# WKV attention, FFN and routed experts on one core: the work ahead of block 0 in another order

## The chip, the cores and the metric

The kernel runs on one core of a Trainium2 chip. The metric is the device time of the program in microseconds, as the median of three runs. TensorE is called PE in the profile, its weight loads PEld, VectorE DVE, ScalarE ACT, GpSimd POOL, and SyncE, which only issues loads and stores here, SP. Each engine works through its own instructions strictly in the order in which the program lists them.

## The reference

Three stages follow one another. First a linear attention with decay, for 4 batches, 8 heads, 768 steps and heads of 48:

```
cur   = outer(u * k[t], v[t])
y[t]  = r[t] @ (state + cur)
state = w[:, None] * state + outer(k[t], v[t])
```

Its output, 3072 tokens of width 384, goes through a gated FFN, `(silu(x @ w_gate) * (x @ w_val)) @ w_out` with an inner width of 1536, whose weights come as 64-bit floats. Last, a router picks one of 8 experts for each token (argmax over `x @ w_gate`), and the expert's `relu(x @ w1) @ w2`, inner width 1024, is scaled by the softmax probability and a sigmoid gate.

## The kernel before, in words

The 3072 tokens are 24 tiles of 128, and three tiles form a block, so that there are 8 blocks. A program written out by hand fixes the order of the instructions on every engine. Ahead of block 0 stands a prologue: it sets constants, builds the tables of the powers of w, computes the attention of tiles 0 to 2, and decodes the FFN weights of the first of twelve groups f. Then `b_block` runs the FFN of each block over its twelve groups, and slots between the groups hold the attention of the next block's tiles, in block 0 also the decoding of the further weight groups. After the blocks come the eight experts.

The steps of the prologue, with the names that the change touches:

- `setup_consts` fills tables and zeros (`wT`, `uT`, `uw`, `rev`, `kr3`, `ident`, `triu`, `mask`, `ones`, `shf`) and starts the first loads. `kr3[i]` takes keys and receptances of tile i, `krT` those of tile 3; they are zeroed first, since a load fills 48 of every 64 partitions. SP issues the loads in the program's order, and a load whose target isn't free holds up those behind it.
- `decay_tables` builds `WT`, the table of powers of w and 1/w, and `uw`, on DVE.
- `a_scale(i)` (L322) multiplies keys and receptances by `WT` on DVE. `a_scores(i)` (L376) forms the scores of a tile in two PSUM banks. `a_same(i)` forms the diagonal: a product on POOL (L325) and four thin sums on TensorE (L328) into bank 7, which `a_same_copy` (L333) takes out. `a_diag(i)` spreads it into a diagonal matrix, on ACT with eight multiplications (L355) or on POOL with one (L357). `a_mask(i)` (L381) puts the masked scores over it, on DVE.
- `a_out_mm(i)` multiplies by the values (L403). The last pair of heads comes first; ACT takes it out (L410), and products with `shf` (L400, the fold products) add it to the other three pairs. `a_out_ev(i)` takes the result out as a rounded part on ACT (L423) and a rest on DVE (L424), which together are `xT`, the FFN's input.
- `conv_steps(f)` decodes the weights of group f in three steps of three DVE instructions (L224 to L226); `conv_a(f)` runs all three. `conv_b(f)` splits them into a rounded part on ACT (L242) and a rest on POOL (L243). `gate_a` transposes the output weights for the router (L251, copy L253).
- `key_table` builds the table `Wk` by which keys enter the state: a product on POOL (L179), four transposes on TensorE (L181), a copy on ACT (L182). `a_keys` (L366) applies it.
- `b_up` (L507) and `b_down` (L526) are the FFN's products. Block 0 starts with the 18 products of `b_up` for group 0.

Most fp32 products show as two records in the trace.

Of the kernel before, what the change touches and what calls it, by code (L numbers as in the profile page):

```python
# [8 lines left out]
F32 = mybir.dt.float32  # L9
# [42 lines left out]
def kernel(  # L52
# [3 lines left out]
    rkv_d: bass.AP,  # L56
    w_d: bass.AP,
    u_d: bass.AP,
    w64_d: bass.AP,
    g_d: bass.AP,  # L60
    w12_d: bass.AP,
# [24 lines left out]
    bad = cst.tile([P, 2 + NF], F32, name="bad")  # L86
    badb = cst.tile([P, 1], BF16, name="badb")
    flag = cst.tile([P, 1], I32, name="flag")
    wT = cst.tile([P, 4], F32, name="wT")
    uT = cst.tile([P, 4], F32, name="uT")  # L90
    uw = cst.tile([P, 4, 2], F32, name="uw")

    right = ctx.enter_context(ExitStack())
# [20 lines left out]
    def bc(ap, axis, shape):  # L114
        return ap.unsqueeze(axis).to_broadcast(shape)
# [4 lines left out]

    def setup_consts():
        dve.memset(wT, 1.0)
        dve.memset(rev, 0.0)
        act.activation(out=rev, in_=rev, func=AF.Silu)
        dve.memset(uT, 0.0)
        dve.memset(uw, 0.0)
        dve.memset(kr3[0], 0.0)
        pool.memset(kr3[1], 0.0)
        for j in range(2):
            sp.dma_start(  # L130
                out=wT[64 * j : 64 * j + HD, :],
                in_=w_d.rearrange("(p j) d -> j d p", j=2)[j],
            )
        a_load_kr(0)
        for j in range(2):
            sp.dma_start(out=uT[64 * j : 64 * j + HD, :], in_=u_d.rearrange("(p j) d -> j d p", j=2)[j])
        dve.memset(kr3[2], 0.0)
        make_identity(nc, ident)
        pool.memset(triu, 1.0)
        pool.affine_select(  # L140
            out=triu, in_=triu, compare_op=ALU.is_gt, fill=0.0, base=0,
            pattern=[[1, P]], channel_multiplier=-1,
        )
        pool.tensor_copy(out=mask, in_=triu)
        pool.memset(ones, 1.0)
        pool.memset(cnt, 0.0)
        pool.memset(spare[4][:, 0 : 6 * P], 0.0)
        for c in range(KC):
            pool.tensor_copy(
                out=shf[:, c].rearrange("s (j m) -> s j m", j=2)[:, :, HD:64],  # L150
                in_=ident.rearrange("s (j m) -> s j m", j=2)[:, :, 16 * c : 16 * c + 16],
            )

    def pair(t, o, step, n):
        return bass.AP(tensor=t.tensor, offset=t.offset + o, ap=[t.ap[0], [P, 4], [step, 2], [1, n]])
# [18 lines left out]
            q = slice(64 * j, 64 * j + 64)  # L174
            dve.tensor_tensor(out=uw[q, :, j], in0=uT[q], in1=pw[q, 0, :, 0], op=ALU.mult)

    def key_table():
        wk2 = kp.rearrange("s h d -> s (h d)").rearrange("s (p t) -> s p t", p=4)
        pool.tensor_tensor(out=wk2, in0=WkT, in1=bc(pw[:, 0, :, 7], 2, [P, 4, P]), op=ALU.mult)  # L179
        for p in range(4):  # L180
            pe.transpose(bank[7][:, p * P : (p + 1) * P], wk2[:, p, :], ident)  # L181
        act.copy(  # L182
            out=Wk.rearrange("s (h d) -> s h d", h=NH),
            in_=bank[7].rearrange("s (h d) -> s h d", h=NH)[:, :, 0:HD],
        )
# [135 lines left out]
        t = kr3[i] if i < 3 else krT  # L321
        dve.tensor_tensor(out=t, in0=t, in1=WT, op=ALU.mult)  # L322

    def a_same(i):
        pool.tensor_tensor(out=pr3[i], in0=kr3[i][:, 0], in1=kr3[i][:, 1], op=ALU.mult)  # L325
        m = bank[7][:, i * 8 : (i + 1) * 8].rearrange("s (j p) -> s p j", j=2)
        for p in range(4):
            pe.matmul(m[:, p], pr3[i][:, p], uw[:, p], start=True, stop=True)  # L328
        a = apool.tile([P, NH], F32, tag="a3", name="a3", bufs=3)
        att[i]["a"] = a  # L330

    def a_same_copy(i, on_act):
        (act.copy if on_act else dve.tensor_copy)(out=att[i]["a"], in_=bank[7][:, i * 8 : (i + 1) * 8])  # L333
# [482 lines left out]
    with tc.manual_schedule():  # L816
# [6 lines left out]
        next_w(1)  # L823
        for i in range(3):
            a_load_part(i, 1)
        sp.dma_start(out=ub, in_=u_d.rearrange("h d -> (h d)").partition_broadcast(P))
        next_w(2)
        sp.dma_start(out=G, in_=g_d)
        decay_tables()
        sc = ((0, 1), (2, 3), (4, 6))  # L830
        for i in range(3):
            a_scale(i)
            a_scores(i, sc[i])
            a_same(i)
        a_same_copy(0, True)
        a_diag(0, True)
        steps = conv_steps(0)
        steps[0]()
        a_same_copy(1, False)
        a_same_copy(2, False)  # L840
        a_diag(1, False)
        a_diag(2, True)
        a_mask(0, sc[0])
        a_out_mm(0, 0, (3,))
        steps[1]()
        conv_b(0, (GV,))
        a_mask(1, sc[1])
        a_out_mm(1, 1, (3,))
        a_out_mm(0, 0, (0, 1, 2))
        a_mask(2, sc[2])  # L850
        a_out_mm(2, 2, (3,))
        a_out_mm(1, 1, (0, 1, 2))
        a_out_ev(0, 0)
        steps[2]()
        a_out_mm(2, 2, (0, 1, 2))
        a_out_ev(1, 1)
        a_out_ev(2, 2)
        gate_a(0)
        conv_b(0, (OUT,))
        key_table()  # L860
        pool.memset(krT, 0.0)
        for i in range(3):
            a_keys(i)
        for b in range(NB):
            pool.memset(Sst[b], 0.0)
        a_load(3)
        a_load_kr(3)
        next_w(3)
        next_w(4)
        conv_a(1)  # L870
        next_w(5)
        a_bonus(3)
        decay_bounds()
# [250 lines left out]
def _layout(inputs):  # L1124
    import numpy as np

    def tiles(a):
        return np.asarray(a).reshape(NB, NH, TPB, P, HD)

    def feat(a):  # L1130
        a = tiles(a).reshape(NB, 4, 2, TPB, P, HD)
        return a.transpose(0, 3, 2, 5, 1, 4).reshape(NT, 2, HD, 4, P)

    def tok(a):
        return tiles(a).transpose(0, 2, 3, 1, 4).reshape(NT, P, DM)

    def word(a):
        return np.ascontiguousarray(a).view(np.int64)

    rows = np.empty((KC, P), dtype=np.int64)  # L1140
    for c in range(KC):
        for j in range(2):
            rows[c, 64 * j : 64 * j + HD] = HD * (2 * c + j) + np.arange(HD)
            rows[c, 64 * j + HD : 64 * j + 64] = HD * (6 + j) + 16 * c + np.arange(16)
    w64 = np.empty((NF, P, FW), dtype=np.int64)
    for i, name in enumerate(("moe_w_gate", "moe_w_val")):
        a = word(inputs[name])[rows].reshape(KC, P, NF, P)
        w64[:, :, i * KC * P : (i + 1) * KC * P] = a.transpose(2, 1, 0, 3).reshape(NF, P, KC * P)
    w64[:, :, 2 * KC * P :] = word(inputs["moe_w_out"]).reshape(NF, P, DM)
    g = np.concatenate([inputs["moe2_w_gate"], inputs["moe2_w_output_gate"]], axis=1)  # L1150
    g = np.ascontiguousarray(g.reshape(KC, P, 16).transpose(1, 0, 2))
    w1 = np.asarray(inputs["moe2_w1"]).reshape(NE, KC, P, NEF, P).transpose(0, 2, 3, 1, 4)
    w2 = np.asarray(inputs["moe2_w2"]).reshape(NE, NEF, P, DM).transpose(0, 2, 1, 3)
    w12 = np.ascontiguousarray(np.concatenate([w1.reshape(NE, P, NEF, DM), w2], axis=3))
    return {
        "krT": np.ascontiguousarray(np.stack([feat(inputs["k"]), feat(inputs["r"])], axis=3)),
        "rkv": np.ascontiguousarray(np.stack([tok(inputs[n]) for n in "rkv"], axis=2)),
        "w": np.ascontiguousarray(inputs["w"]), "u": np.ascontiguousarray(inputs["u"]),
        "w64": w64, "g": g, "w12": w12,
    }  # L1160

# [20 lines left out]
```

## Time and profile before

| What | Value |
|---|---|
| median of 3 runs | 872.16 us (870.61 to 872.62) |
| the profiled execution's own time | 870.71 us |
| its span | 869.0 us |
| busy share of the span | PE 95%, PEld 92%, DVE 52%, ACT 31%, POOL 30% |
| PE's busy tenths in the first four of 40 slices | 5, 7, 7, 8 (then 8, 8, 9 and nearly always 9) |

The span is the time from the first to the last instruction of the profiled execution. A slice is a fortieth of it, 21.7 us, so the prologue is about the first two. A busy share is an average over stages with different limits: what decides in the prologue has to be read from the timelines of the engines there, which give for each group of instructions its start, its length, and the idle time of the engine before it with what ended that idle time.

### The profile page before, as it was taken

The page shows a single profiled execution, that of the slowest core. Times are in us where ns is not written, and L with a number is a line of the kernel's source. Part 1 is how long each engine was busy: PE and PEld are TensorE (multiplying, and loading weights), DVE is VectorE, ACT ScalarE, POOL GpSimd, SP SyncE. Part 2 cuts the span into 40 slices and gives each one's busy share as a digit, 9 for nine tenths or more (in the row PEclk, how much of TensorE's full clock was granted, in tenths as well). Part 3 has the DMA queues.
Part 4 walks back from the last instruction along what each step waited for, and adds up shares of the span by engine and source line. Part 5 has one row for each costly group of instructions (what it writes and reads, how often), then busy time and mean ns, then how long its engine had stood idle before and what let it go on. Part 6 is the DMA issues. An engine that isn't in the chain of part 4 may idle for free.

```text
span 869.0 us, 13916 instructions
## 1 busy us (share of the span) xinstructions
PE 828.9 (95%) x5451; PEld 797.9 (92%) x5451; DVE 456.1 (52%) x946; ACT 271.1 (31%) x591; POOL 262.4 (30%) x237
## 2 busy tenths in 40 slices
PE   5778889999999999999999999999999999999996
PEld 4377879999999999999999999899999999999996
DVE  5497792444456455455545535234575655555541
ACT  0433432211222222212211222223354444444432
POOL 4286565324244245245243312010110210121022
PEclk9999989999999999999999999999999999999999
DMA  8053432681323323323333210410295443434200
GB/s 279 31 209 128 182 109 60 186 216 48 118 87 127 112 100 129 114 101 128 114 101 129 60 46 19 147 51 22 101 355 165 135 162 117 165 136 167 84 25 35
DMA packets 30424, 104.30 MB, mean 120 GB/s; under 512 B 5591, under 2 KB 15377, under 8 KB 27280
## 3 DMA queue, kind: packets, MB, share of 16 engines
q1 hardware_dynamic: 27024, 93.78, 33.3%
q0 software_dynamic: 3328, 9.56, 2.9%
q8 instruction: 45, 0.74, 0.3%
q14 instruction: 27, 0.22, 0.1%
HBM read 85.25 MB, written 16.41 MB: 117 GB/s over the span
## 4 chain that ended last, share of the span: by engine, by line
PE 83%; DVE 6%; issue 2%; ACT 2%; DMA 1%; SPq 1%; POOL 1%; POOLq 0%; DVEq 0%; ACTq 0%
PE bank L507 31%; PE bank L526 17%; PE bank L721 12%; PE bank L738 12%; PE bank L376 2%; PE bank L403 2%; PE bank L389 2%; DVE bank L225 1%; DVE bank L224 1%; PE bank L686 1%; PE bank L752 1%; DVE cv L226 1%; SPq L428 1%; DVE s L516 1%; PE bank L440 1%
## 5 line engine op out<-in xcount | busy, mean ns | idle before, releaser
L507 PE MATMUL bank<-xT,W 128*128 128x384 f32 x1728 | 330.3, 341 | 1.6 <-DMA xT<-stage 1.6
L507 PEld LDWEIGHTS bank<-xT,W 128*128 128x128 f32 x1728 | 304.9, 189 | 5.5 <-DMA xT<-stage 2.5
L526 PE MATMUL bank<-W,h 128*128 128x400 f32 x864 | 177.5, 350 | 0.0
L526 PEld LDWEIGHTS bank<-W,h 128*128 128x128 f32 x864 | 157.1, 191 | 0.6 <-issue 0.2
L518 ACT CAST h<-s 128x384 fp32r<-128x384 f32 x96 | 49.2, 513 | 324.8 <-DVE s L516 324.8
L516 DVE TENSOR_TENSOR s<-s,bank 128x384 f32<-128x384 f32 x96 | 53.1, 554 | 162.0 <-PE bank L507 148.9
L738 PE MATMUL bank<-hd,wf 128*128 128x416 f32 (+1 forms) x576 | 114.1, 344 | 0.0
L738 PEld LDWEIGHTS bank<-hd,wf 128*128 128x128 f32 x576 | 104.5, 189 | 0.6 <-DVE hd L725 0.2
L760 POOL DMA_INDIRECT out_dram<-yo,ix x32 | 34.1, 1067 | 201.5 <-DVE yo L756 175.3
L357 POOL TENSOR_TENSOR at<-ident,a 128x1024 f32<-128x1024 f32 x19 | 36.0, 1897 | 148.6 <-PE bank L507 118.6
L519 DVE TENSOR_TENSOR h<-s,h 128x384 fp32r<-128x384 f32 x84 | 53.0, 631 | 48.6 <-ACT h L518 48.6
L725 DVE SCALAR_TENSOR_TENSOR hd<-bank,hd 128x416 fp32r<-128x416 f32 (+1 forms) x64 | 36.6, 573 | 77.1 <-ACT hd L724 77.1
L670 DVE TENSOR_TENSOR wf<-raw,wf 128x768 fp32r<-128x768 f32 x64 | 61.2, 957 | 7.0 <-ACT wf L669 1.2
L515 ACT ACTIVATE s<-bank 128x384 f32<-128x384 f32 x96 | 47.2, 491 | 47.7 <-PE bank L507 47.6
L721 PE MATMUL bank<-xd1h,wf 128*128 128x416 f32 x192 | 58.2, 360 | 0.0
L724 ACT ACTIVATE hd<-bank 128x416 fp32r<-128x416 f32 (+1 forms) x64 | 32.3, 505 | 82.3 <-PE bank L721 81.8
L588 POOL DMA_INDIRECT xs<-rows,slot x24 | 23.7, 987 | 113.5 <-DVE slot L586 51.5
L669 ACT CAST wf<-raw 128x768 fp32r<-128x768 f32 x64 | 52.8, 825 | 0.0
L381 DVE COPY_PREDICATED at<-mask,bank 128x512 f32<-128x512 int32 x42 | 28.5, 734 | 38.6 <-POOL at L357 35.3
L721 PE MATMUL bank<-xd0h,wf 128*128 128x416 f32 x144 | 43.8, 362 | 0.0
L243 POOL TENSOR_TENSOR W<-cv,W 128x1152 fp32r<-128x1152 f32 (+2 forms) x14 | 32.2, 2304 | 20.3 <-ACT W L242 20.3
L721 PEld LDWEIGHTS bank<-xd1h,wf 128*128 128x128 f32 x192 | 36.1, 189 | 0.4
(178 smaller groups left out, 936.9 us busy)
## 6 DMA issues: line engine op xcount, KB each, us to landing
raw<-in_w_dram SPq DMA_DIRECT2D x36, 768.0 KB, 4.4
raw<-in_w_dram SPq DMA_DIRECT2D x22, 1152.0 KB, 7.5
rkv<-in_rkv_dram SPq DMA_DIRECT2D x21, 576.0 KB, 5.5
krT<-in_krT_dram SPq DMA_DIRECT2D x42, 192.0 KB, 3.4
xs<-zt SPq DMA_DIRECT2D x32, 197.0 KB, 5.6
xr<-xs SPq DMA_DIRECT2D x6, 591.0 KB, 5.7
spare<-in_w_dram SPq DMA_DIRECT2D x2, 1152.0 KB, 8.2
xT<-stage SPq DMA_DIRECT2D x42, 48.0 KB, 2.1
```

Source lines behind the costliest of these rows:

```text
L357: pool.tensor_tensor(out=af, in0=bc(ident, 1, [P, NH, P]), in1=bc(a, 2, [P, NH, P]), op=ALU.mult)
L507: pe.matmul(ps[i], W[f][:, wl, o : o + P], x[:, xl, c, :], start=(c == 0 and n == 0), stop=(c == KC - 1 and n == 2),)
L515: act.activation(out=s, in_=g, func=AF.Silu)
L516: dve.tensor_tensor(out=s, in0=s, in1=v, op=ALU.mult)
L518: act.copy(out=h[:, 0], in_=s)
L519: (pool if blk == 0 else dve).tensor_tensor(out=h[:, 1], in0=s, in1=h[:, 0].bitcast(F32), op=ALU.subtract)
L526: pe.matmul(bank[t][:, 0 : DM + 16], h[:, hl, t * P : (t + 1) * P], W[f][:, wl, 2 * KC * P :], start=(f == 0 and n == 0), stop=(f == NF - ...
L669: act.copy(out=wf[:, 0], in_=raw[:, f])
L670: dve.tensor_tensor(out=wf[:, 1], in0=raw[:, f], in1=wf[:, 0].bitcast(F32), op=ALU.subtract)
L721: pe.matmul(ps, wf[:, wl, c * P : (c + 1) * P], xd[xl][:, c, 0:n], start=(i == 0), stop=(i == 3 * KC - 1))
L725: dve.scalar_tensor_tensor(h[:, 1, 0:n], ps, 0.0, h[:, 0, 0:n].bitcast(F32), ALU.max, ALU.subtract)
L738: pe.matmul(bank[c][:, 0:n], wf[:, wl, o : o + P], h[:, hl, 0:n], start=(f == 0 and i == 0), stop=(f == NEF - 1 and i == 2),)
```

## The change

The order of the prologue's instructions is changed on each engine. w and u come in one array `wu` and in two loads instead of four. The zeros of `krT` and of the states `Sst` are set at the start instead of ahead of block 0; the loads of tile 3 are moved ahead with them. `key_table` is cut in two, and both parts stand before the first value products. The decoding of weight group 1 is spread over the prologue, where it followed it. `pe_warm` is new: it multiplies the table of ones by itself, 384 columns at a time, into a part of bank 7, and nothing uses the results, 24 times at the start and 10 times between the scores.

```diff
@@ -56,6 +56,7 @@
     rkv_d: bass.AP,
     w_d: bass.AP,
     u_d: bass.AP,
+    wu_d: bass.AP,
     w64_d: bass.AP,
     g_d: bass.AP,
     w12_d: bass.AP,
@@ -86,8 +87,8 @@
     bad = cst.tile([P, 2 + NF], F32, name="bad")
     badb = cst.tile([P, 1], BF16, name="badb")
     flag = cst.tile([P, 1], I32, name="flag")
-    wT = cst.tile([P, 4], F32, name="wT")
-    uT = cst.tile([P, 4], F32, name="uT")
+    wuT = cst.tile([P, 2, 4], F32, name="wuT")
+    wT, uT = wuT[:, 0], wuT[:, 1]
     uw = cst.tile([P, 4, 2], F32, name="uw")
 
     right = ctx.enter_context(ExitStack())
@@ -120,20 +121,16 @@
 
     def setup_consts():
         dve.memset(wT, 1.0)
+        dve.memset(uT, 0.0)
+        for j in range(2):
+            sp.dma_start(out=wuT[64 * j : 64 * j + HD], in_=wu_d[j])
+        dve.memset(kr3[0], 0.0)
         dve.memset(rev, 0.0)
         act.activation(out=rev, in_=rev, func=AF.Silu)
-        dve.memset(uT, 0.0)
+        pool.memset(ones, 1.0)
+        a_load_kr(0)
+        pool.memset(kr3[1], 0.0)
         dve.memset(uw, 0.0)
-        dve.memset(kr3[0], 0.0)
-        pool.memset(kr3[1], 0.0)
-        for j in range(2):
-            sp.dma_start(
-                out=wT[64 * j : 64 * j + HD, :],
-                in_=w_d.rearrange("(p j) d -> j d p", j=2)[j],
-            )
-        a_load_kr(0)
-        for j in range(2):
-            sp.dma_start(out=uT[64 * j : 64 * j + HD, :], in_=u_d.rearrange("(p j) d -> j d p", j=2)[j])
         dve.memset(kr3[2], 0.0)
         make_identity(nc, ident)
         pool.memset(triu, 1.0)
@@ -142,7 +139,6 @@
             pattern=[[1, P]], channel_multiplier=-1,
         )
         pool.tensor_copy(out=mask, in_=triu)
-        pool.memset(ones, 1.0)
         pool.memset(cnt, 0.0)
         pool.memset(spare[4][:, 0 : 6 * P], 0.0)
         for c in range(KC):
@@ -150,6 +146,13 @@
                 out=shf[:, c].rearrange("s (j m) -> s j m", j=2)[:, :, HD:64],
                 in_=ident.rearrange("s (j m) -> s j m", j=2)[:, :, 16 * c : 16 * c + 16],
             )
+        pool.memset(krT, 0.0)
+        for b in range(NB):
+            pool.memset(Sst[b], 0.0)
+
+    def pe_warm(n, b=7):
+        for _ in range(n):
+            pe.matmul(bank[b][:, P:], ones, bc(ones, 1, [P, 3, P]), start=True, stop=True)
 
     def pair(t, o, step, n):
         return bass.AP(tensor=t.tensor, offset=t.offset + o, ap=[t.ap[0], [P, 4], [step, 2], [1, n]])
@@ -174,9 +177,12 @@
             q = slice(64 * j, 64 * j + 64)
             dve.tensor_tensor(out=uw[q, :, j], in0=uT[q], in1=pw[q, 0, :, 0], op=ALU.mult)
 
-    def key_table():
-        wk2 = kp.rearrange("s h d -> s (h d)").rearrange("s (p t) -> s p t", p=4)
+    wk2 = kp.rearrange("s h d -> s (h d)").rearrange("s (p t) -> s p t", p=4)
+
+    def key_table_a():
         pool.tensor_tensor(out=wk2, in0=WkT, in1=bc(pw[:, 0, :, 7], 2, [P, 4, P]), op=ALU.mult)
+
+    def key_table_b():
         for p in range(4):
             pe.transpose(bank[7][:, p * P : (p + 1) * P], wk2[:, p, :], ident)
         act.copy(
@@ -321,13 +327,14 @@
         t = kr3[i] if i < 3 else krT
         dve.tensor_tensor(out=t, in0=t, in1=WT, op=ALU.mult)
 
-    def a_same(i):
+    def a_same_a(i):
         pool.tensor_tensor(out=pr3[i], in0=kr3[i][:, 0], in1=kr3[i][:, 1], op=ALU.mult)
+
+    def a_same_b(i):
         m = bank[7][:, i * 8 : (i + 1) * 8].rearrange("s (j p) -> s p j", j=2)
         for p in range(4):
             pe.matmul(m[:, p], pr3[i][:, p], uw[:, p], start=True, stop=True)
-        a = apool.tile([P, NH], F32, tag="a3", name="a3", bufs=3)
-        att[i]["a"] = a
+        att[i]["a"] = apool.tile([P, NH], F32, tag="a3", name="a3", bufs=3)
 
     def a_same_copy(i, on_act):
         (act.copy if on_act else dve.tensor_copy)(out=att[i]["a"], in_=bank[7][:, i * 8 : (i + 1) * 8])
@@ -823,51 +830,60 @@
         next_w(1)
         for i in range(3):
             a_load_part(i, 1)
+        next_w(2)
         sp.dma_start(out=ub, in_=u_d.rearrange("h d -> (h d)").partition_broadcast(P))
-        next_w(2)
         sp.dma_start(out=G, in_=g_d)
+        a_load(3)
+        a_load_kr(3)
+        pe_warm(24)
         decay_tables()
         sc = ((0, 1), (2, 3), (4, 6))
         for i in range(3):
             a_scale(i)
-            a_scores(i, sc[i])
-            a_same(i)
+            a_same_a(i)
+        steps = conv_steps(0) + conv_steps(1)
+        a_scores(0, sc[0])
+        pe_warm(4)
+        a_scores(1, sc[1])
+        a_same_b(0)
         a_same_copy(0, True)
         a_diag(0, True)
-        steps = conv_steps(0)
+        pe_warm(3)
+        a_scores(2, sc[2])
+        a_same_b(1)
+        a_same_copy(1, True)
+        pe_warm(3)
+        a_same_b(2)
+        key_table_a()
         steps[0]()
-        a_same_copy(1, False)
-        a_same_copy(2, False)
-        a_diag(1, False)
-        a_diag(2, True)
-        a_mask(0, sc[0])
-        a_out_mm(0, 0, (3,))
         steps[1]()
         conv_b(0, (GV,))
+        a_diag(1, True)
+        a_mask(0, sc[0])
+        a_same_copy(2, False)
+        a_diag(2, False)
+        key_table_b()
+        a_out_mm(0, 0, (3,))
+        steps[2]()
+        conv_b(0, (OUT,))
         a_mask(1, sc[1])
         a_out_mm(1, 1, (3,))
         a_out_mm(0, 0, (0, 1, 2))
         a_mask(2, sc[2])
         a_out_mm(2, 2, (3,))
+        a_out_ev(0, 0)
         a_out_mm(1, 1, (0, 1, 2))
-        a_out_ev(0, 0)
-        steps[2]()
+        steps[3]()
+        a_out_ev(1, 1)
+        steps[4]()
         a_out_mm(2, 2, (0, 1, 2))
-        a_out_ev(1, 1)
+        gate_a(0)
+        steps[5]()
         a_out_ev(2, 2)
-        gate_a(0)
-        conv_b(0, (OUT,))
-        key_table()
-        pool.memset(krT, 0.0)
         for i in range(3):
             a_keys(i)
-        for b in range(NB):
-            pool.memset(Sst[b], 0.0)
-        a_load(3)
-        a_load_kr(3)
+        next_w(4)
         next_w(3)
-        next_w(4)
-        conv_a(1)
         next_w(5)
         a_bonus(3)
         decay_bounds()
@@ -1137,6 +1153,7 @@
     def word(a):
         return np.ascontiguousarray(a).view(np.int64)
 
+    wu = np.stack([inputs["w"], inputs["u"]])
     rows = np.empty((KC, P), dtype=np.int64)
     for c in range(KC):
         for j in range(2):
@@ -1156,6 +1173,7 @@
         "krT": np.ascontiguousarray(np.stack([feat(inputs["k"]), feat(inputs["r"])], axis=3)),
         "rkv": np.ascontiguousarray(np.stack([tok(inputs[n]) for n in "rkv"], axis=2)),
         "w": np.ascontiguousarray(inputs["w"]), "u": np.ascontiguousarray(inputs["u"]),
+        "wu": np.ascontiguousarray(wu.reshape(2, 4, 2, HD).transpose(2, 3, 0, 1)),
         "w64": w64, "g": g, "w12": w12,
     }
 
```

## Rows read from the trace of the kernel before

**Rows 1.** The page's first line.
```profile
span 869.0 us, 13916 instructions
...
```

**Rows 2.** Chain that ended last, 0 to 140 us: start us, us, what.
```profile
...
43.56 1.01 POOL kp L179
...
45.74 5.22 PE bank L507 x18
...
55.37 0.36 DVE S L454
...
126.83 2.07 PE bank L376 x14
...
```

**Rows 3.** Timeline of DVE, 0 to 75 us: start, us, instruction, idle before and releaser.
```profile
...
8.23 2.36 DVE L322 TENSOR_TENSOR spare<-spare,WT 128x1024 f32<-128x1024 f32 x2
10.87 1.94 DVE L322 TENSOR_TENSOR spare<-spare,WT 128x1024 f32<-128x1024 f32 x1 [0.27 <-DMA spare<-in_krT_dram]
13.39 0.56 DVE L224 TENSOR_SCALAR bank<-raw 128x384 int32<-128x384 int32 x1 [0.59 <-DMA raw<-in_w_dram]
...
21.49 0.24 DVE L333 COPY a<-bank 128x8 f32<-128x8 f32 x2 [6.35 <-ACT a L333]
...
26.32 2.55 DVE L381 COPY_PREDICATED spare<-mask,bank 128x512 f32<-128x512 int32 x4
...
41.29 0.56 DVE L424 TENSOR_TENSOR xT<-bank,xT 128x384 fp32r<-128x384 f32 x1 [3.42 <-ACT xT L423]
...
46.98 0.45 DVE L188 TENSOR_TENSOR wT<-wT,pw 128x4 f32<-128x4 f32 x1
...
```

**Rows 4.** Timeline of TensorE's products, 0 to 75 us.
```profile
...
9.52 2.08 PE L376 MATMUL bank<-spare 64*128 64x128 f32 x16 [9.52 <-DVE spare L322]
11.78 1.87 PE L328 MATMUL bank<-uw,spare 128*128 128x2 f32 x8 [0.19 <-POOL spare L325]
...
27.09 1.28 PE L403 MATMUL bank<-spare 128*48 128x128 f32 x4 [1.62 <-DVE spare L381]
...
40.66 0.90 PE L251 MATMUL bank<-ident,cv 128*128 128x128 f32 x3
...
45.39 5.57 PE L507 MATMUL bank<-xT,W 128*128 128x384 f32 x18
...
54.82 1.85 PE L507 MATMUL bank<-xT,W 128*128 128x384 f32 x9
...
60.02 1.16 PE L376 MATMUL bank<-krT 64*128 64x128 f32 x16
...
65.52 0.55 PE L251 MATMUL bank<-ident,cv 128*128 128x128 f32 x3 [2.56 <-DVE at L381]
66.63 0.90 PE L259 MATMUL bank<-G,gt 128*128 128x16 f32 x6 [0.57 <-ACT gt L253]
...
```

**Rows 5.** Windows: length, busy of PE, PEld, DVE, ACT, POOL, PEclk, DMA share, GB/s.
```profile
...
28.00:32.00 4.00, 4.00 (x20) 2.32 (x20) 0.87 (x2) 0.52 (x2) 1.50 (x1) 1.00 0.01 4
...
65.00:70.00 5.00, 3.92 (x17) 3.66 (x18) 4.76 (x9) 2.06 (x5) 4.62 (x4) 0.73 0.00 2
...
```

**Rows 6.** Timeline of SP's queue, 0 to 75 us: issues of loads.
```profile
...
3.07 0.91 SPq L136 DMA_DIRECT2D uT<-in_u_dram  x2
...
45.49 0.79 SPq L308 DMA_DIRECT2D krT<-in_krT_dram  x2
...
```

**Rows 7.** Timeline of POOL, 0 to 75 us.
```profile
...
9.55 5.62 POOL L325 TENSOR_TENSOR spare<-spare 128x512 f32<-128x512 f32 x3 [4.88 <-DVE spare L322]
...
44.51 0.95 POOL L861 MEMSET krT<- 128x1024 f32 x1
...
49.28 1.92 POOL L865 MEMSET S<- 128x512 f32 x4
...
```

**Rows 8.** Timeline of ACT, 0 to 75 us.
```profile
...
21.56 4.78 ACT L355 ACTIVATE spare<-ident,a 128x128 f32<-128x128 f32 x16
...
40.78 0.48 ACT L423 CAST xT<-bank 128x384 fp32r<-128x384 f32 x1 [3.50 <-PE bank L403]
...
```

## The prediction

> **What bounds the kernel now.** I read the page first, then the chain of waits, then the timeline of each engine over the first 75 us, and last the windows for the clock. The span is 869.0 us and the profiled execution took 870.71 us, so 1.7 us lie around the span [rows 1]; the median of the three runs is 872.16, which is 1.45 above it. From about 127 us on TensorE carries the chain nearly alone. Ahead of that the reader should see one handover: the chain runs through the key table on POOL (43.56) to TensorE's first product of block 0 at about 45.4, through its 18 products, and on to DVE at 55.37 [rows 2]; from there DVE (decoding weights) carries most of it until TensorE takes over at 126.83. So block 0 cannot start before 45.4, and every microsecond by which it starts earlier on TensorE and on DVE is one off the end, as long as nothing in the block has a due time of its own. Its weight loads follow buffers that DVE frees, so they move along.
>
> Before 45.4 the engines mostly wait for one another. DVE waits 6.35 us ahead of the copies at 21.49 and 3.42 us ahead of 41.29 [rows 3]. TensorE's first product is at 9.52, and its products of the prologue are slow: 16 records of the scores take 2.08 us there and 1.16 us at 60.02; the 18 up-products take 5.57 us (0.31 each) at 45.39, against 1.85 for 9 (0.21, its tail counted) at 54.82 [rows 4]. That is TensorE at 1.2 against 2.4 GHz, the two levels of its clock. The clock column shows 1.00 in the window 28 to 32 [rows 5], but there the product durations contradict it, and I go by the durations. The long run is 27.09 to 41.56 (40.66 + 0.90) [rows 4]: value and fold products almost without a pause for 14.5 us, and no sign that the clock rose.
>
> **The change part by part.**
>
> *Loads.* w and u come in two loads instead of four. Two issues of together 0.91 us leave SP's queue [rows 6], and what is behind them lands up to 0.9 earlier. DVE waits 0.27 and 0.59 for those loads [rows 3], 0.86 in all; between nothing and 0.86 I take 0.6: the first decode step starts at 12.8 instead of 13.39. The krT load of tile 3, which stands at 45.49 in SP's queue behind POOL's memset [rows 6], and with it all later weight loads, is issued some 30 us earlier. That costs the path nothing and is no gain, since no row of DVE's timeline between 47 and 75 us names a load. The later loads now wait in SP for buffers that DVE and TensorE free; weight 3 is issued when the last value product ends (35.7 below), about 11 us before the 46.3 at which the krT issues end today [rows 6], while block 0 moves by less.
>
> *Zeros and ones.* The memsets of krT (0.95) and S (1.92) go from 44.51 and 49.28 to POOL's start [rows 7]. POOL has nothing between its setup and 9.55, so the cover is that wait. They stand beside DVE's small table operations, which no row shows beside a memset. Bounds: nothing, to their own 2.87 if they held DVE up throughout. The only slowing seen is a product beside a product: the third scale takes 1.94 against 1.18 for each of the first two [rows 3]. A memset is further from that than from the conversion work beside which it stood at 44.51, so I take nothing.
>
> *Products with ones.* 24 products of 384 columns start once the ones exist, about 1 us in, while TensorE waits until 9.5 anyway. The nearest row is 0.31 for 384 columns at 1.2 GHz [rows 4]: 24 x 0.31 = 7.4 us, ended by 8.6 at the latest. At that same rate the 18 up-products at 45.39 ended in a clock at 2.4 GHz, since the next ones run at 0.21. So I expect the fast clock for the scores. Ten more products follow in between, 1.7 us at the fast rate, all in waits. They write bank 7, where the diagonal sums stand, so they wait for the copies of these: the second group of three waits for the copy of tile 1, queued in ACT behind eight multiplications, 4.78/2 = 2.4 us [rows 8].
>
> *Up to the second mask.* DVE: 12.8, two decode steps of 1.75 (three rows of 0.55 to 0.56 with short pauses, the first of them shown) to 16.3, mask 0 (2.55/2 = 1.28) to 17.6 [rows 3]. It then waits for the diagonal of tile 2. That comes so: POOL's first product ends at about 11.5 (the three take 5.62 from 9.55, [rows 7]), TensorE's sums of tile 0 follow the scores of tile 1 and end at 13.2, ACT's copy and multiplications end at 15.9, the next copy at 16.1, three ones-products at 16.7, sums of tile 2 (1.87/2 = 0.93) at 17.7 [rows 4, 8]. DVE's copy ends at 18.0, the third decode step at 19.8, mask 1 at 21.1. TensorE's long run starts at 21.2 instead of 27.09: **5.9 us** gained.
>
> *The long run.* 14.5 us at 1.2 GHz. At 2.4 GHz about half. Which? From 16.7 to 21.2 TensorE would have only the thin sums (2 columns), four transposes, two value products, and at least 2 us of nothing. The nearest case: at 65.52 an idle stretch of 2.56 us ends in three transposes, then 0.57 idle and six products of 16 columns [rows 4], and in the window 65 to 70 the granted clock is 0.73, a mix of its two levels [rows 5], although the scores at 60.02 had run at the fast one. I take the slow clock: 21.2 + 14.5 = 35.7, since the same run did not raise it before.
> The Trainium skill (TensorE: Matmul & The Clock Gate, section Why this matters for your kernels) warns only of longer gaps between bursts than any here; by it the clock would hold, and the time would be that of the rival "the clock holds" below. The fall after 2.56 us and thin products does not agree with it.
>
> *From there to block 0.* Before, 3.83 us pass from 41.56 to 45.39: the key table, which now lies in front, and is hidden between 15 and 20 us behind DVE's decoding and ACT's multiplications. Its cost if it was not hidden: the 1.8 us from POOL's start at 43.56 [rows 2] to 45.39, and ACT's copy. In its place the gate copy stands ahead of tile 2's eviction on ACT: 0.48 + 0.48, then DVE's 0.56 [rows 3, 8], 1.5 us. Block 0 starts at 37.2, its 18 products take 5.4 us as before: gain on TensorE 5.9 + 3.8 - 1.5 = **8.2 us**.
>
> *DVE.* The decoding of weight 1 (5.2 us, three steps) ran from behind the eviction at 41.29 to 46.98 and now fills waits between 22 and 36. DVE is through at 37.2 against 46.98 [rows 3], 9.8 earlier. That is more than TensorE gains, and DVE meets TensorE's work again at 55.37 [rows 2], where the chain goes over, so 8.2 decides. ACT's and POOL's work ahead of block 0 only moves forward.
>
> Sum: 870.71 - 8.2 = 862.5 for an execution like the profiled one, 872.16 - 8.2 = 864.0 as a median.
>
> **The rivals.**
>
> *The clock holds* at 2.4 GHz through the long run. For it: the ones-products fill some of the waits, and between 54.82 and 61 the clock stayed fast with pauses and thin products among the wide ones [rows 4]. Against it: the fall near 66 [rows 4, 5]. The run takes 7.3 and ends at 28.5. Then DVE binds: ACT evicts tile 0 at 25.3, and DVE does three evictions and three steps after it, 3 x 0.56 + 3 x 1.75 = 6.9, to 32.2. DVE is 46.98 - 32.2 = 14.8 earlier; TensorE starts at 32.3 and needs 3.5 instead of 5.4, 15 earlier. 872.2 - 14.8 = 857.4.
>
> *The ones do not raise the clock* (the change doesn't do what it is for). Then scores, sums and the ten ones-products (3.1) stand in a row on TensorE from 9.5 with ACT's 2.4 us between: sums of tile 2 end at 24.9, mask 1 at 28.1, run until 42.7, block 0 at 44.2. Gain 1.2: 871.0, no change that could be measured. Against it: 18 products of the same width did raise it.
>
> *Slower: the clock stays at 1.2 GHz far into block 0.* Since the rise would have to come in the 18 up-products, and the thinner products behind them could miss it. At half clock TensorE's products cost up to twice: at most 0.5 us lost for each us. Point from which it decides: 8.2/0.5 = 16 us of slow clock on the path more than before. 30 us more would give 872.2 - 8.2 + 15 = 879. Against it: at 45.39 the rise came within the 18 products [rows 4], and the fall near 66 left the window 65 to 70 with a mean of 0.73 only [rows 5].
>
> **How the numbers follow.** Forecast (8.2 us, ±2 for where in the block the clock falls, for the waits between engines and for the memsets): 0.66. The clock holds: 0.17. In between, part of the run fast, 858 to 862: 0.07. No rise: 0.06. Slower: 0.04. The likeliest is 864.0. The range takes in the first three: 856.5 to 867. A difference of 0.2% (1.7 us) is about what a measurement of this kernel can tell from none. Faster by more than that: 0.66 + 0.17 + 0.07 + 0.02 of "no rise" = 0.92; same: the rest of it and the edge of the slow case, 0.05; slower 0.03.
>
> **What would show it.** Scores of 16 records in about 1.2 us at 9.5; ACT's first copy of the sums near 13.3 instead of 21.3; the run of value and fold products from about 21 to 36 with the fold product at the old pace; no key table behind it; the 18 up-products from about 37 to 42.5; DVE's next decode at about 38. If the run takes 7 to 8 us, the clock held and the time is near 857. If the scores take 2.08 us, the ones did nothing. If block 0 begins at 37 but ends less than 8 us earlier, the block had a due time or a slow clock that I did not see.

## The result, and the profile after

The changed kernel takes 862.22 us (median of 4 runs, 861.38 to 866.78) against 871.92 before: ratio 0.9899, interval 0.9866 to 0.9931. Measured again with more executions the ratio is 0.9893 (0.9878 to 0.9908), which is 9.3 us of 871.6. The forecast was 864.0, a gain of 8.2.

To read the profile one has to know that it is of the slowest execution, 866.78 us (span 865.1): of eleven executions of this kernel the two profiled ones took 866.8 and 867.1, the nine others 861.0 to 863.3. What differs is shown below. First TensorE's timeline of the profiled execution, columns as in [rows 4], which it answers to:

```profile
...
1.16 5.56 PE L155 MATMUL bank<-ones 128*128 128x384 bf16 x24 [1.16 <-POOL ones L130]
9.51 1.16 PE L383 MATMUL bank<-spare 64*128 64x128 f32 x16 [2.78 <-DVE spare L328]
...
11.59 2.08 PE L383 MATMUL bank<-spare 64*128 64x128 f32 x16
...
26.13 1.27 PE L410 MATMUL bank<-spare 128*48 128x128 f32 x4 [0.52 <-DVE spare L388]
...
39.70 0.90 PE L257 MATMUL bank<-ident,cv 128*128 128x128 f32 x3
41.56 5.21 PE L514 MATMUL bank<-xT,W 128*128 128x384 f32 x18 [0.95 <-ACT xT L430]
...
61.77 0.55 PE L257 MATMUL bank<-ident,cv 128*128 128x128 f32 x3 [3.00 <-DVE at L388]
...
64.19 3.35 PE L533 MATMUL bank<-W,h 128*128 128x400 f32 x9
...
```

Windows of the same execution, columns as in [rows 5]. The third value from the end, PEclk, is the granted clock (1.00 is 2.4 GHz, 0.50 is 1.2):

```profile
...
5.00:11.00 6.00, 3.22 (x30) 2.06 (x29) 5.77 (x21) 0.00 (x0) 3.89 (x6) 1.00 0.99 275
12.00:26.00 14.00, 12.69 (x70) 10.17 (x68) 7.81 (x15) 6.61 (x22) 7.87 (x5) 0.50 0.90 329
26.00:41.00 15.00, 14.47 (x65) 8.11 (x65) 7.87 (x15) 3.12 (x9) 5.81 (x6) 0.50 0.28 88
...
46.00:62.00 16.00, 11.95 (x122) 10.46 (x121) 13.68 (x25) 6.90 (x16) 10.77 (x9) 1.00 0.12 49
63.00:69.00 6.00, 6.00 (x21) 5.97 (x22) 3.71 (x7) 0.77 (x3) 2.98 (x3) 0.50 0.17 43
...
```

The ones raise the clock: the scores of tile 0 take 1.16 us, as in block 0, where they took 2.08 before [rows 4]. But the 24 products are done after 5.56 us, at 6.7, because they run fast themselves from about 4.2 us on. TensorE then pauses for 2.78 us. At 11.05 us the clock falls, and the scores of tile 1 take 2.08 again. The ones-products that follow run slowly and stand in the way: value products start at 26.13, 0.96 ahead of [rows 4], and take 14.5 us to 40.60. Even so block 0 starts at 41.56 instead of 45.39. The clock falls a second time in block 0, at the place where it fell before (61.77 answers to 65.52 in [rows 4]: 3.00 us of pause, then thin products); the nine down-products at 64.19 take 3.35 us.

DVE, answering to [rows 3]:

```profile
...
8.22 4.56 DVE L328 TENSOR_TENSOR spare<-spare,WT 128x1024 f32<-128x1024 f32 x3
12.71 0.55 DVE L230 TENSOR_SCALAR bank<-raw 128x384 int32<-128x384 int32 x1
...
23.62 0.17 DVE L340 COPY a<-bank 128x8 f32<-128x8 f32 x1 [4.65 <-PE bank L336]
...
42.01 0.15 DVE L194 TENSOR_TENSOR wuT<-wuT,pw 128x4 f32<-128x4 f32 x1
...
```

The three scales need 4.56 us without a pause, and the first decode step starts at 12.71 instead of 13.39. The copy of the third diagonal waits 4.65 us for the slow sums. DVE is done with the prologue at 42.01 instead of 46.98. ACT and POOL, answering to [rows 8] and [rows 7]:

```profile
...
15.50 0.17 ACT L340 COPY a<-bank 128x8 f32<-128x8 f32 x1 [13.06 <-PE bank L336]
...
40.64 0.48 ACT L259 COPY gt<-bank 128x384 f32<-128x384 f32 x1 [4.32 <-PE bank L257]
41.02 0.48 ACT L430 CAST xT<-bank 128x384 fp32r<-128x384 f32 x1
...
```

```profile
...
4.62 0.95 POOL L149 MEMSET krT<- 128x1024 f32 x1
5.50 1.92 POOL L151 MEMSET S<- 128x512 f32 x4
...
15.12 1.05 POOL L183 TENSOR_TENSOR kp<-WT,pw 128x512 f32<-128x512 f32 x1
...
```

ACT's first copy of the sums comes at 15.50; before, it waited for all three sums. The gate copy and the last eviction stand where they were expected. POOL's zeros lie in its wait, and the key table's product at 15.12.

### The profile page after: what moved, and what is told of

It reads as the page before. It is cut to its first block, busy times and chain, and to the rows that moved or that the text cites. A ratio compares the mean times of both kernels' runs of the same rounds, so it can differ in the third digit from the quotient of the medians.

```text
span 865.1 us, 13982 instructions
## 1 busy us (share of the span) xinstructions
PE 836.2 (97%) x5485; PEld 801.3 (93%) x5485; DVE 455.0 (53%) x945; ACT 271.5 (31%) x592; POOL 263.6 (30%) x237
## 4 chain that ended last, share of the span: by engine, by line
PE 88%; DVE 6%; issue 2%; ACT 2%; DMA 0%; POOL 0%; SPq 0%; POOLq 0%; DVEq 0%; ACTq 0%
PE bank L514 32%; PE bank L533 17%; PE bank L728 12%; PE bank L745 12%; PE bank L383 3%; PE bank L410 3%; PE bank L396 2%; DVE bank L231 1%; DVE bank L230 1%; PE bank L693 1%; PE bank L759 1%; DVE cv L232 1%; PE bank L407 1%; PE bank L447 1%; PE bank L336 1%
## 5 line engine op out<-in xcount | busy, mean ns | idle before, releaser
L344 POOL TENSOR_TENSOR rkv<-rkv,ub 128x384 f32<-128x384 f32 x21 | 21.3, 1017 | 46.9 <-DMA rkv<-in_rkv_dram 46.9
```

## The experiments

Unless said otherwise a kernel is the changed one with the edit shown. Each was timed four to twelve times; ratios are against the kernel before, timed on the same chip. The "ones" are the products of `pe_warm`. A profile is of one execution.

**The same kernel again.** 

> The changed kernel, unaltered, in a second look. Theory A (the place where the clock falls differs from execution to execution, and the profiled one, 866.8 us, is an early fall: clock down at 11.05 us, value products from 26.1, block 0 from 41.6): other executions fall later, start the value products near 21 and block 0 near 37, and take 861 to 863. A profile that lands on such an execution shows the scores of all three tiles in 1.2 us each and ACT's first copy of the sums near 13.4. Rival B (the order of the engines gives the time, the clock's place in the prologue does not matter): every execution has its value products near 26, and 866.8 is a stray.

Measured: 862.46 (861.04 to 867.11), ratio 0.9893. The profile again caught one near 867: clock down at 10.9 us, value products at 26.3, block 0 at 41.69, 867.1. The other five took 861.0 to 863.3 with a mean granted clock of 0.975 to 0.978 over the span, against 0.970 for the profiled one. So there are two kinds; that the clock of the kind near 862 falls later had still to be seen. Both slow executions are the profiled ones; whether that is chance stays open.

**36 ones instead of 24.**

```diff
-        pe_warm(24)
+        pe_warm(36)
```

> The changed kernel with 36 products of ones at the start instead of 24, so that TensorE has no pause of 2.8 us ahead of the scores; all else stays. Theory A (the pause ahead of the scores lets the clock fall early in some executions): no execution falls before the sums, value products from about 21, median 862 and the highest below 864. If the 12 further products run at the slow clock they end up to 2 us after 9.5 and cost that. Rival (the early fall has another cause, the thin sums): some executions at 866 remain.

Measured: 861.42 (861.08 to 862.67), ratio 0.9889 (0.9875 to 0.9903), mean clock 0.976 to 0.978, none near 867. TensorE and its windows:

```profile
...
1.17 8.49 PE L155 MATMUL bank<-ones 128*128 128x384 bf16 x36 [1.17 <-POOL ones L130]
9.58 1.16 PE L383 MATMUL bank<-spare 64*128 64x128 f32 x16
...
12.52 1.05 PE L336 MATMUL bank<-uw,spare 128*128 128x2 f32 x8
...
20.86 1.29 PE L410 MATMUL bank<-spare 128*48 128x128 f32 x4 [1.22 <-DVE spare L388]
...
34.45 0.90 PE L257 MATMUL bank<-ident,cv 128*128 128x128 f32 x3
36.30 5.39 PE L514 MATMUL bank<-xT,W 128*128 128x384 f32 x18 [0.95 <-ACT xT L430]
...
```

```profile
...
7.00:19.00 12.00, 11.07 (x102) 8.34 (x100) 10.95 (x19) 5.03 (x17) 8.41 (x6) 1.00 1.02 348
20.00:35.00 15.00, 14.14 (x65) 8.11 (x65) 8.55 (x16) 3.19 (x10) 7.16 (x7) 0.50 0.62 195
...
```

With no pause ahead of the scores the clock stays up to the diagonal sums (1.05 for eight, 1.87 in [rows 4]). The value products start at 20.86 where the forecast had 21.2, still run slowly, and end at 35.35 where it had 35.7. Block 0 starts at 36.30. Theory A's forecast holds: by time and mean clock none of the five took the early fall, nor did any of the 17 executions of the four kernels below that have 36 ones and the same work on TensorE up to the sums. All five profiles show the clock up until 19.3 us or later. That it is the pause which makes the kind near 867 isn't shown alone, since 36 ones close the pause and make the run of ones longer. By time and mean clock the nine executions near 862 are like this one; none of them was profiled.

**No ones.** All four `pe_warm` calls out. 

> The changed kernel without any product of ones; all else stays. Theory A (the ones raise the clock for scores and sums, worth 2 to 3 us where the fall comes late): the clock stays down until the up-products. Scores and sums then stand in a row on TensorE from 9.5 to about 21.3, mask 1 starts near 23.4, the value products near 24, block 0 near 40, time 865 to 866.5. Rival B (the order does it all): 862, as the changed kernel. Rival C (without the ones most of the gain is gone): 870 or more.

Measured: 864.48 (863.33 to 864.73), ratio 0.9917 (0.9904 to 0.9931), 3.1 us behind the kernel with 36 ones on the same chip. TensorE:

```profile
...
23.70 1.27 PE L410 MATMUL bank<-spare 128*48 128x128 f32 x4 [0.52 <-DVE spare L388]
...
39.12 6.40 PE L514 MATMUL bank<-xT,W 128*128 128x384 f32 x18 [0.95 <-ACT xT L430]
...
```

Theory A, half a microsecond below its range. Value products at 23.70, 3.4 us ahead of [rows 4] by the order alone, block 0 at 39.12. This is faster than the profiled execution of the changed kernel, 866.8 us with block 0 at 41.56: there the ones cost more than they brought.

**Only ones.** The kernel before, with the table of ones made first and 24 products ahead of the scores. 

> The kernel before, with the table of ones made first on POOL and 24 products of ones ahead of the scores; no other part of the change. Theory A: scores and sums end up to 4.4 us earlier than 21.3 where the clock holds through them, nearer 1 us where it falls at about 11; the long run stays slow and the key table stands on the path: 868 to 871. Rival (the clock is the whole gain): 862.

Measured: 871.39 (869.59 to 872.95), ratio 0.9997 (0.9986 to 1.0007): nothing.

```profile
...
9.53 1.16 PE L380 MATMUL bank<-spare 64*128 64x128 f32 x16 [2.97 <-DVE spare L326]
11.78 1.87 PE L332 MATMUL bank<-uw,spare 128*128 128x2 f32 x8 [1.09 <-POOL spare L329]
...
27.10 1.28 PE L407 MATMUL bank<-spare 128*48 128x128 f32 x4 [1.62 <-DVE spare L385]
...
```

The scores of tile 0 are fast, the clock falls as they end (10.7 us), TensorE waits for POOL, and up to block 0 the rest is as before to two hundredths. All twelve executions have a mean clock of 0.965 to 0.969, like the profiled one (0.967). The smallest gain that theory A gave was one microsecond; it was none, and the time lies 0.4 above its range.

**The decoding of weight 1 back behind the last eviction** (with 36 ones).

```diff
-        steps[3]()
         a_out_ev(1, 1)
-        steps[4]()
...
-        steps[5]()
         a_out_ev(2, 2)
...
+        for u in steps[3:]:
+            u()
```

> The changed kernel with 36 products of ones at the start, and the three decode steps of weight 1 put back behind the last eviction, as one piece ahead of block 0. TensorE's work of the prologue stays as it is. Theory A (DVE and TensorE both set block 0; DVE has only about 1.9 us to spare there): DVE is 5.3 us later at block 0, 3.4 of it count, 864.5 to 865.5. Rival B (TensorE's start of block 0 alone decides): 861.4, as with the steps in the waits.

Measured: 862.66 (861.46 to 863.85), ratio 0.9892 (0.9877 to 0.9908), the same as with the steps in the waits (0.9889). DVE's first instruction of weight groups 1, 2 and 4, and under it, for groups 2 and 4, that with the steps in the waits:

```profile
...
36.67 0.55 DVE L230 TENSOR_SCALAR bank<-raw 128x384 int32<-128x384 int32 x1
...
42.15 0.55 DVE L230 TENSOR_SCALAR bank<-spare 128x384 int32<-128x384 int32 x1
...
59.57 0.57 DVE L230 TENSOR_SCALAR bank<-raw 128x384 int32<-128x384 int32 x1
...
```

```profile
...
37.02 0.55 DVE L230 TENSOR_SCALAR bank<-spare 128x384 int32<-128x384 int32 x1
...
56.50 0.57 DVE L230 TENSOR_SCALAR bank<-raw 128x384 int32<-128x384 int32 x1
...
```

Group 2 starts 5.1 us later and group 4 still 3.1 us later, about the 3.4 that theory A said would count. Group 5 starts at 69.16 (69.03): the delay is gone. In this profile the clock fell at 50.2 and was up again at 57.0, while DVE carried the work; with the steps in the waits it fell at 57.4 to 64.2, and DVE waited 3.17 us for TensorE. So in this one profile theory A's delay is there, and the clock fell at a place where it cost less; that the same holds in the other executions isn't shown. On the timed runs the move is worth nothing that can be measured.

**The key table back behind the last eviction** (with 36 ones).

```diff
-        key_table_a()
...
-        key_table_b()
...
         a_out_ev(2, 2)
+        key_table_a()
+        key_table_b()
```

> The changed kernel with 36 products of ones at the start, and both parts of the key table put back behind the last eviction. Theory A (the 3.8 us of the key table before came from POOL, which stood behind ACT's late split of the weights; now POOL is free by then, and only the four transposes, which wait for the gate copy, stand ahead of the first up-product): 0.5 to 1.1 us later, 862 to 862.5. Rival B (as in my sum: its place is worth the whole 3.8 us): 865.

Measured: 861.52 (860.38 to 862.63), ratio 0.9872 (0.9855 to 0.9889): no loss.

```profile
...
35.95 1.09 PE L187 MATMUL bank<-ident,kp 128*128 128x128 f32 x4 [0.66 <-ACT gt L259]
36.69 5.01 PE L514 MATMUL bank<-xT,W 128*128 128x384 f32 x18
...
```

The transposes at 35.95 fill the time in which the first up-product would wait for the eviction. Block 0 starts 0.4 us later. Rival B, my sum's term, falls; the time is below theory A's range as well.

**The key table and the split of group 0's output weights back** (with 36 ones). As above, and `conv_b(0, (OUT,))` between the last eviction and the key table. 

> The changed kernel with 36 products of ones at the start, both parts of the key table behind the last eviction, and also the split of the output weights of group 0 (ACT's rounded part, POOL's rest) put back between that eviction and the key table. Theory A (the 3.8 us ahead of block 0 came from POOL's late rest and ACT's late rounding, with the key table's product queued behind them): ACT's rounding near 36.4, POOL's rest near 37, the product near 38, block 0 near 39.7 instead of 36.3, and 864.5 to 865.5. Rival B (the key table's place alone, already tried, is all there is): 861.5 to 862.

Measured: 865.46 (864.63 to 866.29), ratio 0.9936 (0.9922 to 0.9950), in theory A's range. TensorE and POOL:

```profile
...
38.70 1.12 PE L187 MATMUL bank<-ident,kp 128*128 128x128 f32 x4 [3.44 <-POOL kp L183]
39.46 5.09 PE L514 MATMUL bank<-xT,W 128*128 128x384 f32 x18
...
```

```profile
...
36.65 0.99 POOL L249 TENSOR_TENSOR W<-cv,W 128x384 fp32r<-128x384 f32 x1 [15.48 <-ACT W L248]
37.59 1.05 POOL L183 TENSOR_TENSOR kp<-WT,pw 128x512 f32<-128x512 f32 x1
...
```

POOL's rest of the output weights ends at 37.64, only then comes the key table's product, and TensorE's transposes wait 3.44 us for it. Block 0 starts at 39.46, 3.2 us later than with both in front. From the end of the value products (35.26) to block 0 it is 4.20 us; before it was 3.83, with the same instruction ahead of the key table's product on POOL (43.56 in [rows 2]):

```profile
...
42.57 0.99 POOL L243 TENSOR_TENSOR W<-cv,W 128x384 fp32r<-128x384 f32 x1 [13.07 <-ACT W L242]
...
```

The split alone, with the key table in front, was not tried.

**Zeros and loads of tile 3 back** (with 36 ones): memsets of `krT` and `Sst`, `a_load(3)` and `a_load_kr(3)` behind the last eviction. 

> The changed kernel with 36 products of ones at the start, and the zeros of krT and of the states and the loads of tile 3 put back behind the last eviction. Theory A (they were and are covered): 861.4, within 0.7. Rival B (the loads of tile 3 and with them the weight loads behind them in SP's queue come too late for block 0): over 863.

Measured: 862.31 (861.61 to 862.56), ratio 0.9883 (0.9868 to 0.9898). The time is 0.2 us above theory A's edge and far from rival B's; the ratio is no higher than that of the kernel with them in front (0.9889).

**Only the order of the sums.** No ones; the key table, output weights, zeros, loads of tile 3 and decoding of weight 1 behind the last eviction as before. 

> Only the order of the diagonal sums, of their copies and of the first decode steps as changed (and the two loads for w and u); no products of ones, and key table, zeros, loads of tile 3, output weights of group 0 and decoding of weight 1 behind the last eviction as before. Theory A (that order alone starts the value products at 23.7 instead of 27.1, and the 3.8 us behind them stay): block 0 near 42, 867.5 to 868.5. Rival B (the parts behind the evictions make the gain): 870 or more.

Measured: 867.93 (866.10 to 868.11), ratio 0.9963 (0.9949 to 0.9977). The time is the expected one. The profiled execution is the fastest of the five (866.10, the others 867.4 to 868.1), and in it block 0 starts at 40.62, 1.4 us earlier than expected: the clock was up from 13.9 to 17.2 us without any ones. The mean clock of the other four (0.989 or 0.990 against 0.974) says that they differ in this.

**Holding the clock through the value products.**

```diff
-        pe_warm(24)
+        pe_warm(36)
...
+        pe_warm(5, 0)
         key_table_b()
         a_out_mm(0, 0, (3,))
+        pe_warm(12, 1)
```

> The changed kernel with 36 products of ones at the start (as in the run that kept the early fall away) and 17 more in the two waits ahead of the value products: 5 into bank 0 behind mask 0, 12 into bank 1 behind the first value products of tile 0. Theory A (the clock falls at 19.9 us because of the thin products and pauses there, and the value products, once fast, keep it): value products at the fast rate, 7 to 8 us instead of 14.5, block 0 near 32 instead of 36.3, and DVE with its decode steps the later one; 857 to 858. Rival B (the value products with their pauses cannot hold the clock): the fall comes a few us later, 859 to 861.5. Rival C (the extra products themselves delay the path): over 862.

Measured: 856.10 (855.99 to 857.06), ratio 0.9812 (0.9799 to 0.9826).

```profile
...
20.90 2.52 PE L155 MATMUL bank<-ones 128*128 128x384 bf16 x12
23.35 0.43 PE L410 MATMUL bank<-spare 128*48 128x128 f32 x4
...
30.89 0.55 PE L257 MATMUL bank<-ident,cv 128*128 128x128 f32 x3
32.39 0.44 PE L514 MATMUL bank<-xT,W 128*128 128x384 f32 x1 [0.95 <-ACT xT L430]
34.09 4.77 PE L514 MATMUL bank<-xT,W 128*128 128x384 f32 x17 [1.26 <-DVE xT L431]
...
```

The granted clock of the run, columns as in [rows 5]:

```profile
...
22.00:31.00 9.00, 9.00 (x72) 5.36 (x71) 4.03 (x8) 2.13 (x7) 5.86 (x6) 1.00 0.77 229
...
```

The run from 23.35 to 31.44 takes 8.1 us instead of 14.5. The clock had fallen at 18.3 and was up again at 21.7, while the twelve ones ran: theory A, 0.9 us below its range, and in this profile by a return, not by holding. The price of my rival "the clock holds" (857.4) is met within 1.3 us. The second up-product waits 1.26 us for DVE's eviction, which stands behind a decode step.

**Evicting first.** As the last one, with `a_out_ev(2, 2)` ahead of `gate_a(0)` and `steps[5]()`. 

> The kernel that held the clock (36 + 17 more products of ones), with the last tile's eviction ahead of the gate's transposes and copy and ahead of the last decode step of weight 1. Theory A (time = start of the first up-products + some 822 to 824; in the run that held the clock they wait 1.26 us for DVE's eviction, which stands behind the decode step, and 0.48 for the gate copy): up-products from about 32 without a pause, 854 to 855. Rival B (DVE, now 0.6 to 1.8 us later with its decoding, takes over as what sets block 0): 856, no gain.

Measured: 855.96 (853.34 to 857.21), ratio 0.9815 (0.9797 to 0.9834): no gain over the last one by the median. The five are far apart: two took 853.3 and 853.4, below theory A's range, three 856.0 to 857.2.

```profile
...
20.25 2.12 PE L155 MATMUL bank<-ones 128*128 128x384 bf16 x12
...
30.49 0.45 PE L514 MATMUL bank<-xT,W 128*128 128x384 f32 x1
...
```

In the profiled execution (856.17) the clock did hold: it was granted in full from 7.5 to 37.5 us, and the twelve ones took 2.12 us instead of 2.52. Block 0 starts 1.9 us earlier than in the last profile. At the first down-product of block 1 1.1 us of that are left, in the span 0.8 (854.5 against 855.3). The clock's last fall in block 0 took 6.8 us (51.5 to 58.3) instead of 3.4 (55.9 to 59.3), but the last kernel's fell once more (42.2 to 45.6), so this alone doesn't explain the loss. DVE starts weight groups 2, 4 and 5 1.2 to 3.2 us earlier than in the last profile: rival B's figure, not its cause. What takes the rest stays open.

**Ones inside block 0.** As the last one, and 14 more products:

```diff
+                slots[4].insert(0, lambda: pe_warm(14, 0))
```

> The kernel that evicts first (36 + 17 more products of ones), with 14 more products of ones inside block 0, into bank 0, in TensorE's pause of 2.7 us ahead of the gate transposes of weight 3, where the clock fell in each profile so far but one. Theory A (that fall costs 1.5 to 2.9 us: DVE's decoding of weights 4 and 5 starts 11.1 to 12.6 us apart where the clock falls between them, and 9.6 apart in the one profile where it fell earlier): decoding of weights 4 and 5 9.6 us apart, 852.5 to 854.5. Rival B (DVE sets that stretch, the slow products are covered): 856, no gain, although the clock holds. Rival C (the products delay what stands behind them): 857 or more.

Measured: 857.05 (856.00 to 860.39), ratio 0.9839 (0.9818 to 0.9859).

```profile
...
48.90 2.45 PE L155 MATMUL bank<-ones 128*128 128x384 bf16 x14
...
53.52 1.89 PE L533 MATMUL bank<-W,h 128*128 128x400 f32 x9
...
```

The clock stays up here: the down-products take 1.89 instead of 3.35, and the decoding of weight groups 4 and 5 starts 9.6 us apart, at 51.55 and 61.14 (12.6 in the last run). TensorE's first down-product of block 1 comes 14.9 us earlier than in the kernel before, 1.9 more than in the last run. Against the last run this is lost later: 0.8 us in block 1, and 2.0 between the first down-products of experts 0 and 1. The longest of TensorE's waits from 300 us to the end:

```profile
...
PE bank L728 <- issue: 1.9, 1, 1.9
...
```

This wait, among the first up-products of expert 1, has no releaser in the profile, and the run before has none such. The time is in rival C's range, but nothing is delayed in block 0: theory A is right there and wrong for the whole. The cause of the 1.9 us was not found, nor whether the other four executions have it.

## Why the prediction was right, and where it was not

*What sets the time.* In the 14 profiles (before, after and the twelve experiments) the span less the start of TensorE's first up-product lies between 822.9 and 824.1 (before 869.0 - 45.4 = 823.6, after 865.1 - 41.6 = 823.5, with 36 ones 860.4 - 36.3 = 824.1). The start itself moves over 14.9 us, from 45.4 to 30.5. The claim that a microsecond at block 0 is a microsecond at the end held, though partly by pieces that cancel: the clock falls at different places in block 0, and the later blocks and experts differ by up to 2 us.

*Loads, zeros.* The first decode step was forecast for 12.8 and came at 12.71 (13.16 with 36 ones, where DVE waited 0.38 us for the load); the zeros cost nothing, the scales start at 8.22 as before. Moving the zeros back cost nothing either.

*Up to the second mask, 5.9 us.* Right with 36 ones: value products at 20.86, 6.2 us gained, of which 3.4 come from the order and 2.8 from the clock (23.70 without ones). In the profiled execution of the changed kernel it was 1.0. The step that failed there is "24 x 0.31 = 7.4 us, ended by 8.6": I took the slow rate for all of them. They ended at 6.7, I did not look for a pause behind them, and the clock fell at 11.05, before the sums. In the executions near 862 time and mean clock speak for a later fall.

*The long run.* At the slow clock, 14.5 us, as forecast. With ones in the two waits ahead of it it took 8.1 us, and the kernel 856.1. That fits the thin work and the pauses there as the cause of the fall; which of the two it is was not separated. With 36 ones the fall came at 19.9 us, behind pauses of 0.42 and 1.22 us only.

*From there to block 0, 3.8 less 1.5 us.* The size was nearly right (2.9, from 3.83 to 0.95, where the sum has 2.3), the cause wrong. I named "the key table, which now lies in front". Its place is worth nothing: put back alone it cost 0.4 us at block 0 and no time that could be measured. The 3.8 us came from the split of group 0's output weights, late on ACT and POOL, behind which the key table's product was queued; with both back 3.2 us of block 0's start were lost. My list of the parts had passed this one over, as it stands in the diff as one moved line. That the term came out is luck: the move that I priced is worth nothing, and one that I hadn't seen is worth as much. The 1.5 was 0.95, because the first product needs only ACT's part of the eviction.

*DVE.* "9.8 earlier" came out as 10.2 with 36 ones (46.98 to 36.75). "So 8.2 decides" leaves DVE 1.6 us to spare. With DVE five microseconds later, 3.1 of them were still there at weight group 4, so the margin is about 2 us; yet the timed runs lost nothing, in the one profile because the clock fell elsewhere.

*The rivals.* No rise of the clock was priced at 871.0 with the ones in the way. The nearest case is the profiled execution, with the clock down from 11 us on: 866.8. Without any ones it is 864.5, so the new order alone carries 7.1 of the 10.2 us that it gains with 36 ones on the same chip. The clock that holds was priced at 857.4 and measured 856.1.

*The sum.* With 36 ones block 0 starts 9.1 us earlier (6.2 and 2.9), and the span is 8.6 shorter; the forecast was 8.2. For the kernel as forecast, with 24 ones, no profile shows an execution near 862, so its terms are taken from the one with 36.

In ratios: the order of the sums and the two loads 0.9963; with key table, output weights, zeros and decoding in front as well 0.9917; with ones that leave no pause 0.9889; with ones ahead of the value products 0.9812.

## What to carry to other kernels

Before a moved step is given a wait as its price, follow the wait back along each queue: what stood late was the instruction in front of the moved one. A filler that raises TensorE's clock should reach up to the work that it is meant for, and its own length has to be taken at both rates: 24 ones were done in 5.4 to 5.6 us and left a pause; 36 took 7.7 to 8.9, and at 8.9 held the scores up by 0.5 us. Ones paid ahead of the 14.5 us of value products (ratio 0.9889 to 0.9812). Among the thin sums, with the clock down, they cost time (866.8 us against 864.5 without any). Where a clock falls at places that differ from execution to execution, one profile can show a kind of execution that most runs are not: compare its time with the median first.

## What the runs showed of the hardware that was not expected

- The value and fold products run at 1.2 GHz for 14.5 us and do not raise the clock, though TensorE is busy for 14.47 of 15 us in the window 26 to 41; the same products, once the clock is at 2.4 GHz, kept it there for 8 us (window 22 to 31: 1.00).
- The clock fell after 2.8 us of pause and one set of scores, and in block 0 after 3.0 us of pause and thin products; with 14 ones in that pause it stayed. With 36 and 17 ones it fell in block 0 after a pause of only 1.5 us (ended at 53.87, fall at 55.9).
- The same run of ones, begun at 1.2 us in each profile that has it, raised the clock at 3.9 us in one and at 7.1 in another.
- 1.9 us of wait on TensorE with no releaser appeared among the products of expert 1 in one profile only, at 628 to 630 us, 580 us behind the only edit that sets that kernel apart.
